# A fused two-branch attention kernel: where single maxima, the last output rows and their sums are placed

## The chip, the cores and the metric

The kernel runs on one core of one Trainium2 chip. The metric is the device time of one execution in microseconds (us); the median of several executions is given. A core has these engines, each with an instruction queue of its own, which they work through in order: TensorE (in the profile PE, with its weight loads as PEld), VectorE (DVE), ScalarE (ACT), GpSimd (POOL) and SyncE (SP, which here only issues transfers). They wait for each other through semaphores alone. Matmul results land in PSUM, eight banks of 128 partitions by 512 fp32 values; the other data lie in SBUF.

## The reference

The input x has 2048 tokens of 512 values. Two attention branches with 32 heads of 16 values work on the same x; a gate per token mixes them.

```python
# branch A: each query looks at 8 keys, at distances 0, 2, ... 14
qkv = (x @ wqkv).reshape(B, S, 3, H, Dh)
logits = einsum("bhsd,bhswd->bhsw", q, k[idx]) * scale      # masked where idx < 0
a = einsum("bhsw,bhswd->bhsd", softmax(logits), v[idx]).reshape(B, S, D) @ wo_a
# branch B: full attention, one key and value head shared by all 32 query heads
q = (x @ wq).reshape(B, S, H, Dh); k = x @ wk; v = x @ wv
p = softmax(einsum("bhqd,bkd->bhqk", q, k) * scale)
b = einsum("bhqk,bkd->bhqd", p, v).reshape(B, S, D) @ wo_b
g = sigmoid((x * gate_w).sum(-1))
out = g * a + (1 - g) * b
```

B_wq and B_wk are drawn eight times larger than the other weights. The scores of branch B are so large that the maximum of each row has to be taken off before the exponential.

## The kernel before

**The main loop.** Branch B is cut into 32 units: four blocks of 512 queries by eight groups of four heads. A unit has 16 steps, one for each 128 keys, so there are 512 steps s = 0 to 511 (`NS`), and one more that only finishes; `u, kt = divmod(s, 16)` gives unit and place in it. A step does `exp_pair(s, 0)` and `exp_pair(s, 1)`: two score products (L473) into one of the two double banks `pe` (`eb`), and one exponential of 128 x 1024 on ScalarE (L475). Then `weighted(s - 1)` (L483) multiplies the exponentials of the step before with the values into the bank `po`, which collects the sum of one unit. Score products use half of TensorE's rows each, so the two of a pair run side by side.

**The maxima.** Before a unit's exponentials start, the maxima of its score rows must be known, since they enter its queries as two further rows (L461, a transfer). They take 2048 half-array products in all, 64 a unit, with TensorE and VectorE working ahead of the exponentials. A *pair* (`fill_pair`, products at L324, reduction at L344) puts two products into the double bank `pm` (`m2`) and reduces 1024 values; a *single* (`fill_one`, reduction at L355) puts one product into the bank `ps` (`m1`). In the front part a third form is used, a *difference pair* (`fill_diff`, `fill_sum`): products of sums and differences of keys at L409, absolute values on ScalarE (L419), and one VectorE operation with a running maximum (L429); one pair of it does four products' worth of maxima for four half-array products. A unit's maxima are collected in a tile `mx`, first filled with the lowest number: in the front part by ScalarE (L318) when a unit is first touched, in the main loop by GpSimd (L315), there for the unit after it as well. Three such tiles rotate.

**The order.** All engines' instruction order is fixed when the program is built, by a planner with its own clocks (`clk`) and costs (`T_R` and the others). In a step the order is `(0, "m2", "m1", 1)`: first score products, a pair of maxima if `m2` is free by the planner's clock, a single if `m1` is free, second score products. Singles are used only while `singles(s)` holds, that is while more maxima are left than pairs alone would do by step 480, and not at a unit's first step (`kt` is 0): there `finish_a` also has VectorE transpose `po` (L497) and take reciprocals (L503) behind `weighted` of the unit that ended. If a unit's maxima are still missing shortly before it starts, `pause` runs what is left through the `pe` banks as well, without exponentials.

**The front.** Before the loop, `stream` runs the projections (`lumps`, products at L1057) on the banks `e0` and `e1` and fills maxima in between; the last lump uses `m2`. The set `ended` stops the filling of `m2` near the end of the lump before it.

**Output rows.** The last 512-wide products with wo_a and wo_b are made in four blocks of four row groups. Three blocks run as `out_phase` at a unit's second step, once branch A (GpSimd's work, `work`) is far enough, the block's units are shaped, and the maxima are less than `LEAD` = 3 units ahead. The last four row groups come in two parts: `spread` makes most of their products (L812, 21 slots of two for each row group, into `m2`) in the last steps of the loop, at most four slots a step (`spread_some`), after a preparation (`prepare` L637 and L639, transposes L783, splits L793 and L795). At the end of a row group ScalarE copies the second bank (L829) and VectorE adds the first (L831), which frees `m2`. The generator is made in the loop once unit 29 is shaped and no maxima are left. What needs the last unit's result comes after the loop in two halves x = 0, 1 (L1170 to L1188): transposes, normalisation, a split in two parts (L1177, L1178), six products, the sum with `parts[j]` (L1187), the store.

Of the kernel before, what the change touches and what calls it, by code (L numbers as in the profile page):

```python
# [6 lines left out]
F32 = mybir.dt.float32  # L7
# [11 lines left out]
NJ = S // P  # L19
C = D // P  # L20
# [28 lines left out]
def gated_mix_kernel(ctx, tc, xt, wa, wk, wq, wo_a, wo_b, out):  # L49
# [36 lines left out]
    def after(eng, ready, dur):  # L86
        clk[eng] = max(clk[eng], ready) + dur
        return clk[eng]
# [219 lines left out]
        return bool(half) or bool(slots) and slots[0][0] < len(stacked) and stacked[slots[0][0]] <= clk["pe"]  # L308

    def unit_tile(v):  # L310
        for x in (v, v + 1) if pe else (v,):
            if x < NU and x not in left:
                mx[x] = wp.tile([P, 2, 2, 4, 4], F32, name="mx", bufs=3)
                if pe:
                    nc.gpsimd.memset(mx[x], -FMAX)  # L315
                    charge(250)
                else:
                    nc.scalar.activation(mx[x].rearrange("p b i t k -> p (b i t k)"), ident[:, 0:64], AF.Identity, scale=0.0, bias=mk[:, 6:7])  # L318
                left[x] = NF // NU
        return mx[v]  # L320
# [455 lines left out]
    def spread(js, n):  # L776

        m = 3 * (C + n)

        def turn_all(j):  # L780
            bank = m1
            for c in range(C):
                nc.tensor.transpose(bank[:, c * P:(c + 1) * P], oa[c // 2][:, j, c % 2 * P:(c % 2 + 1) * P], ident)  # L783
            after("pe", 0, 0.7)
            own = p2[0].tile([P, C, P], F32, name="raw", bufs=1)
            nc.scalar.activation(own, bank.rearrange("p (c q) -> p c q", c=C), AF.Copy)
            after("act", clk["pe"] + T_LAT, 0.6)
            return own

        def parts_a(j, own):  # L790
            nonlocal pool
            hi, lo = turned[j, 0] = [pe[0].tile([P, C, P], F32R, name=f"turned{x}", bufs=1) for x in range(2)]
            nc.scalar.activation(hi, own, AF.Copy)  # L793
            at = after("act", clk["pe"], 0.6)
            nc.gpsimd.tensor_sub(lo, own, hi.bitcast(F32))  # L795
            pool = max(pool, 1e3 * at) + 1300

        prepare(js[0], n)
        yield 1.0
        parts_a(js[0], turn_all(js[0]))  # L800
        yield 3.0
        while slots or half:
            yield 1.0
        for j in js:
            nxt = j + 1 if j != js[-1] else None
            items = []
            for i in range(m):
                items = items or out_items(j, n)
                st, mv = items[i]
                for b in range(2):  # L810
                    h = slice(64 * b, 64 * b + 64)
                    nc.tensor.matmul(m2[:, b, :], st()[h], mv[h], start=(i == 0), stop=(i == m - 1))  # L812
                after("pe", 0, T_R)
                row_left[0] = m - 1 - i
                if i == 3 * n and nxt:
                    prepare(nxt, n)
                if i == m - 8 and nxt:
                    raw = turn_all(nxt)
                if i < m - 1:
                    yield 0.0  # L820
            del turned[j, 0], turned[j, 1]
            x = len(parts)
            if x < 2:
                spare.append(p2[0].tile([P, 512], F32, name="part", tag=("own", "tr8")[x], bufs=1))
            elif x == 2:
                two = p2[0].tile([P, 2, 512], F32, name="part", tag="pr", bufs=1)
                spare.extend([two[:, 0, :], two[:, 1, :]])
            parts[j] = spare[x]
            nc.scalar.activation(parts[j], m2[:, 1, :], AF.Copy)  # L829
            after("dve", after("act", clk["pe"] + T_LAT, 0.5), 0.7)  # L830
            nc.vector.tensor_add(parts[j], m2[:, 0, :], parts[j])  # L831
            if nxt:
                parts_a(nxt, raw)
            yield 1.5
        done.add("last")

    def spread_some(k):
# [222 lines left out]
    def done_mm(at):  # L1060
        nonlocal pool
        x, i = at
        lump = lumps[x]
        if i % 3 == 2:
            run_tasks()
            if p2:
                run_pool()
        if x == last - 1 and i == 3 * C - 2:
            ended.add(1)
        if x == last and i in (2, 7):  # L1070
            exp_pair(0, int(i == 2))
        if i < 3 * C - 1:
            return
        if lump[0] == "q":
            m = lump[1]
            queries_post(m, eb[x % 2])
            free[f"e{x % 2}"] = clk["act"]
            ahead_wa(0, m - 4)
        else:
            gg, j = lump[1:]  # L1080
            a_post(gg, j, 2 if x == last else x % 2)
            if gg + 1 < C:
                ahead_wa(gg + 1, j - 2)
# [22 lines left out]
    for s in range(NS + 1):  # L1106
# [16 lines left out]
        order = (0, "m2", "m1", 1) if s > 1 else (1, "m2", 0, "m1") if s else ()  # L1123
        k, n = outs // 4, C - (outs >= NJ - 4)
        if outs == NJ - 4:
            if NU - 3 in shaped and not half and not singles(s) and not later_rows and "last" not in done:
                later_rows.append(spread(list(range(outs, NJ)), n))
            if short > 0 and steps < 2:
                pause(short)
        elif due or outs < NJ and s and kt == 0 and outs // NH in done and NHG * (k + 1) - 1 in shaped and (lead < LEAD or s >= 16 * (NHG * (k + 2) + 1)):  # L1130
            if not due:
                prepare(outs, n)
                due.append(n)
            else:
                out_phase(list(range(outs, outs + 4)), due.pop(), kt == 1)
                outs += 4
                order = (0, "m1", 2)
        elif short > 0 and steps < 2:
            pause(short)

        for which in order:
            if which == "m2":
                fill_ready("m2", M2S)
            elif which == "m1":
                if not later_rows and (kt or not s) and singles(s):
                    fill_ready("m1", M1S)
            elif s < NS:
                exp_pair(s, which % 2 or which // 2, which == 2)
# [17 lines left out]
    for x in range(2):  # L1166
# [8 lines left out]
        nc.vector.transpose(own, obp["t"][:, 8 * x:8 * x + 8].rearrange("p b h d -> p (b h d)"))  # L1175
        tl = wp.tile([P, 2, 256], F32R, name=f"tl{x}", tag="aext", bufs=2)
        nc.scalar.activation(tl[:, 0], own, AF.Copy)  # L1177
        nc.gpsimd.tensor_sub(tl[:, 1], own, tl[:, 0].bitcast(F32))  # L1178
        tls.append(tl)
    for x in range(2):  # L1180
        for k, w in ((0, woh), (0, wol), (1, woh)):
            for t in range(2):
                nc.tensor.matmul(eb[x][:, t, :], tls[x][:, k, t * P:(t + 1) * P], w[1][:, C - 1, :], start=(w is woh and k == 0), stop=(k == 1))
        for t in range(2):
            j = NJ - 4 + 2 * x + t
            os = px.tile([P, D], F32, name="osl", tag="pexp", bufs=6)
            nc.vector.tensor_add(os, eb[x][:, t, :], parts[j])  # L1187
            (nc.sync, nc.scalar)[t].dma_start(out[0].rearrange("(p j) d -> p j d", j=NJ)[:, j, :], os)  # L1188
# [29 lines left out]
```

## Time and profile before

| | |
|---|---|
| median of three executions | 1504.08 us (1503.17 to 1506.13) |
| profiled execution | 1503.76 us, span 1502.0 us |
| mean granted TensorE clock | 0.997 |
| front part, up to the first product into po | 274.2 us |
| TensorE, share of the span | 98% |
| ScalarE | 86% |
| VectorE | 79% |
| GpSimd | 68% |

The span runs from the first to the last instruction; the profiled execution took 1.76 us more. A line of groups or of the timeline names the source line, the engine, the operation, the tile written and the tiles read, their shapes and the count; in brackets stands how long the engine was idle before it, and who released it. The busy time of matmuls is modelled at its ends, so that a busy TensorE is not at its peak rate; the distance from one start to the next tells more. The granted clock is the share of full speed that TensorE was given.

### The profile page before, as it was taken

The numbers are of one execution on the slowest core, as the hardware profiler recorded it, in microseconds if no ns is written. First come the engines' busy times: TensorE is split into PE (matmuls) and PEld (weight loads), VectorE is DVE, ScalarE is ACT, GpSimd is POOL, SyncE is SP. The second block draws the span as 40 slices with busy tenths as digits, with TensorE's granted clock in tenths as the row PEclk, the third lists the DMA queues.
The fourth block names the chain that finished last, engine by engine and source line by source line (L and its number), as shares of the span: only waits on it lengthen the run. The fifth ranks groups of instructions, "written<-read, shape, count | busy, mean of one in ns | idle before, by whom it ended". The sixth has DMA issues, their size and how long they took to land.

```text
span 1502.0 us, 29449 instructions
## 1 busy us (share of the span) xinstructions
PE 1479.2 (98%) x11020; PEld 710.5 (47%) x11020; DVE 1188.4 (79%) x1814; ACT 1285.7 (86%) x1672; POOL 1024.8 (68%) x1806
## 2 busy tenths in 40 slices
PE   9999999999999999999999999999999999999998
PEld 6899888433333333333733345333333463333343
DVE  6976666788888888888788888888888888888801
ACT  5568988899999999999899988999989889999785
POOL 7876988788888888988988799788897130111021
PEclk9999999999999999999999999999999999999999
DMA  6754223121120211211212112021120000000000
GB/s 219 212 147 143 76 87 117 33 83 46 60 84 12 73 58 41 70 41 41 69 41 70 41 41 87 12 70 41 41 76 16 12 30 12 2 1 2 1 2 28
DMA packets 44287, 87.75 MB, mean 58 GB/s; under 512 B 9520, under 2 KB 25952, under 8 KB 39920
## 3 DMA queue, kind: packets, MB, share of 16 engines
q1 hardware_dynamic: 37136, 46.89, 10.3%
q0 software_dynamic: 6432, 37.94, 7.5%
q8 instruction: 86, 1.41, 0.4%
q10 hardware_dynamic: 576, 1.05, 0.2%
q14 instruction: 57, 0.47, 0.1%
HBM read 59.02 MB, written 26.30 MB: 57 GB/s over the span
## 4 chain that ended last, share of the span: by engine, by line
PE 91%; ACT 5%; DVE 2%; issue 1%; DMA 0%; POOL 0%; SPq 0%; DVEq 0%; ACTq 0%; POOLq 0%
PE po L483 33%; PE pe L473 25%; PE pe L1057 8%; PE pm L324 8%; PE ps L324 5%; PE pe L740 4%; PE pm L409 2%; ACT dd L419 2%; ACT pexp L475 1%; PE ps L409 1%; PE pm L812 1%; PE po L409 1%; PE pe L183 1%; DMA xraw<-xt 0%; DVE mx L344 0%
## 5 line engine op out<-in xcount | busy, mean ns | idle before, releaser
L475 ACT ACTIVATE pexp<-pe 128x1024 f32<-128x1024 f32 x1021 | 987.3, 1023 | 106.0 <-PE pe L473 103.6
L344 DVE TENSOR_REDUCE mx<-pm 128x2 f32<-128x1024 f32 x508 | 620.0, 1221 | 147.4 <-PE pm L324 139.6
L483 PE MATMUL po<-pexp,vst 128*32 128x512 f32 x4096 | 546.6, 606 | 0.0
L473 PE MATMUL pe<-qst,kst 64*128 64x512 f32 x1914 | 520.4, 455 | 5.6 <-DVE mx L344 2.9
L473 PEld LDWEIGHTS pe<-qst,kst 64*128 64x128 f32 x1914 | 213.3, 184 | 424.6 <-ACT pexp L475 410.2
L355 DVE TENSOR_REDUCE mx<-ps 128x1 f32<-128x512 f32 x446 | 303.1, 680 | 2.1 <-PE ps L324 2.1
L324 PE MATMUL pm<-kst,qst 62*128 62x512 f32 x968 | 196.8, 398 | 2.9 <-DVE mx L344 2.1
L543 POOL TENSOR_TENSOR pr<-aext 128x256 f32<-128x256 f32 x256 | 182.6, 741 | 3.4 <-DMA aext<-ad 3.1
L324 PE MATMUL ps<-kst,qst 62*128 62x512 f32 x422 | 177.3, 420 | 0.5 <-DVE mx L355 0.3
L603 POOL TENSOR_TENSOR oa<-oa,av 128x256 f32<-128x256 f32 x224 | 164.5, 734 | 14.9
L483 PEld LDWEIGHTS po<-pexp,vst 128*32 128x32 f32 x4096 | 80.6, 108 | 174.5 <-issue 166.6
L600 POOL TENSOR_TENSOR av<-aext,lg 128x256 f32<-128x256 f32 x224 | 139.7, 623 | 12.5
L324 PEld LDWEIGHTS ps<-kst,qst 62*128 62x128 f32 x422 | 77.5, 184 | 68.3 <-DVE mx L355 64.9
L1057 PE MATMUL pe<-wah,xl 64*128 64x384 f32 (+1 forms) x504 | 108.9, 338 | 0.0
L419 ACT ACTIVATE dd<-pm 128x512 f32<-128x512 f32 x166 | 92.0, 608 | 19.6 <-PE pm L409 9.5
L1057 PE MATMUL pe<-wah,xh 64*128 64x384 f32 (+1 forms) x504 | 108.6, 337 | 0.0
L1057 PE MATMUL pe<-wal,xh 64*128 64x384 f32 (+1 forms) x504 | 108.3, 337 | 0.0
L429 DVE CUSTOM_DVE_ANT_0 dd<-ps,dd 128x512 f32<-128x512 f32 x83 | 57.4, 692 | 58.4 <-PE ps L409 25.4
L324 PEld LDWEIGHTS pm<-kst,qst 62*128 62x128 f32 x968 | 93.2, 187 | 8.0 <-DVE mx L344 3.4
L509 POOL TENSOR_TENSOR rl<-rl,gate_t 128x16 f32<-128x16 f32 x31 | 6.9, 222 | 118.2 <-DVE rl L503 118.1
L549 POOL TENSOR_TENSOR tr<-pr 128x512 f32<-128x512 f32 x64 | 81.7, 1277 | 4.1
L549 POOL TENSOR_TENSOR tr<-tr 128x256 f32<-128x256 f32 (+1 forms) x128 | 72.5, 567 | 9.0
(215 smaller groups left out, 1908.1 us busy)
## 6 DMA issues: line engine op xcount, KB each, us to landing
aext<-ad POOLq DMA_DIRECT2D x32, 1056.0 KB, 5.5
ad<-stage SPq DMA_DIRECT2D x32, 384.0 KB
qst<-qd SPq DMA_DIRECT2D x60, 128.0 KB
xraw<-xt SPq DMA_DIRECT2D x16, 256.0 KB
qd<-qhi SPq DMA_DIRECT2D x16, 256.0 KB
qd<-qlo SPq DMA_DIRECT2D x16, 256.0 KB
qst<-qd SPq DMA_DIRECT2D x60, 64.0 KB
qst<-ml SPq DMA_DIRECT2D x216, 2.0 KB
```

The lines of the kernel that those rows point to most:

```text
L324: nc.tensor.matmul(dst, qst[home(v)[0]][b:b + 62, pr, t * P:(t + 1) * P], kst[b:b + 62, kc * 512:(kc + 1) * 512], start=True, stop=True)
L344: nc.vector.tensor_reduce(m[:, :, pr, t, kc], dst, AX.X, ALU.max)
L355: nc.vector.tensor_reduce(m[:, odd, pr, t, kc:kc + 1], dst, AX.X, ALU.max)
L419: nc.scalar.activation(dd[0][:, odd], m2[:, odd, :], AF.Abs)
L473: nc.tensor.matmul(bank[:, odd, :], kst[b:b + 64, kt * P:(kt + 1) * P], qst[home(u)[0]][b:b + 64, pr, :], start=True, stop=True)
L475: nc.scalar.activation(e, bank, AF.Exp, scale=SCALE)
L483: nc.tensor.matmul(po[32 * i:32 * i + 32, :], vst[:, kt, :], pexp[s, i // 2][:, i % 2, :], start=(kt == 0), stop=(kt == NJ - 1))
L543: nc.gpsimd.tensor_mul(pr[:, k], q, e[:, o:o + NH, AC:2 * AC])
L549: nc.gpsimd.tensor_add(nx, cur[:, :, 0:n], cur[:, :, n:2 * n])
L600: nc.gpsimd.tensor_mul(av, e[:, o:o + NH, 2 * AC:].rearrange("p j (h d) -> p j h d", d=DH), lg[:, w].unsqueeze(3).to_broadcast([P, NH, AG, ...
L603: nc.gpsimd.tensor_add(ao, ao, av)
L1057: nc.tensor.matmul(front[2 if x == last else x % 2][0][:, b, :n], l[h], r[h], start=(i == 0), stop=(i == 3 * C - 1))
```

## The change

- A unit's first step may have a single of maxima too: `(kt or not s)` leaves the condition.
- The generator of the last rows is made once at most nine maxima products are left, not only when none is left. It prepares its first row group, and begins products when no maxima are left. Once it is made there are no singles.
- At the end of a row group VectorE copies the second bank and then adds the first; ScalarE does no copy. For the last row group ScalarE still copies, and VectorE's addition moves behind the loop, between the two halves of the tail.
- In the tail's second half VectorE does the subtraction of the split, not GpSimd.
- In the front part too, touching a unit fills the `mx` tile of the next one.
- In the last lump but one, the filling of `m2` stops at i = 6 and not at i = 10.

```diff
     def unit_tile(v):
-        for x in (v, v + 1) if pe else (v,):
+        for x in (v, v + 1):
             if x < NU and x not in left:
...
             parts[j] = spare[x]
-            nc.scalar.activation(parts[j], m2[:, 1, :], AF.Copy)
-            after("dve", after("act", clk["pe"] + T_LAT, 0.5), 0.7)
-            nc.vector.tensor_add(parts[j], m2[:, 0, :], parts[j])
             if nxt:
+                nc.vector.tensor_copy(parts[j], m2[:, 1, :])
+                nc.vector.tensor_add(parts[j], m2[:, 0, :], parts[j])
                 parts_a(nxt, raw)
-            yield 1.5
+                after("dve", clk["pe"] + T_LAT, 1.4)
+                yield 1.5
+            else:
+                nc.scalar.activation(parts[j], m2[:, 1, :], AF.Copy)
         done.add("last")
...
-        if x == last - 1 and i == 3 * C - 2:
+        if x == last - 1 and i == 3 * C - 6:
             ended.add(1)
...
-            if NU - 3 in shaped and not half and not singles(s) and not later_rows and "last" not in done:
+            if NU - 3 in shaped and to_go() <= 9 and not later_rows and "last" not in done:
                 later_rows.append(spread(list(range(outs, NJ)), n))
...
-                if not later_rows and (kt or not s) and singles(s):
+                if not later_rows and singles(s):
                     fill_ready("m1", M1S)
...
-        nc.gpsimd.tensor_sub(tl[:, 1], own, tl[:, 0].bitcast(F32))
+        (nc.vector if x else nc.gpsimd).tensor_sub(tl[:, 1], own, tl[:, 0].bitcast(F32))
         tls.append(tl)
+        if not x:
+            nc.vector.tensor_add(parts[NJ - 1], m2[:, 0, :], parts[NJ - 1])
```

## The prediction

> **What bounds the kernel now.** I read the page's totals and chain first, then busy time by stretches, then the timeline at the places that the change touches.
>
> ```profile
> PE 1479.2 (98%) x11020; PEld 710.5 (47%) x11020; DVE 1188.4 (79%) x1814; ACT 1285.7 (86%) x1672; POOL 1024.8 (68%) x1806
> PE 91%; ACT 5%; DVE 2%; issue 1%; DMA 0%; POOL 0%; SPq 0%; DVEq 0%; ACTq 0%; POOLq 0%
> ```
>
> TensorE is busy 98% of the 1502.0 us and carries 91% of the chain, so a matmul slot that is added costs time, and one that is filled sideways saves only idle time. The stretches (columns: time, then busy us and instructions of PE, PEld, DVE, ACT, POOL, then the granted clock, DMA) show where idle time is left:
>
> ```profile
> 274.00:1398.00 1124.00, 1120.03 (x7992) 439.49 (x7993) 961.09 (x1301) 1016.04 (x1155) 788.92 (x1468) 1.00 0.13 43
> 1417.50:1424.00 6.50, 3.29 (x20) 1.65 (x21) 5.09 (x6) 1.32 (x3) 0.00 (x0) 0.72 0.00 1
> ```
>
> In the main loop PE idles 4 us in 1124. One hole stands out: 1417.5 to 1424, where the unfinished maxima of the last unit are forced and PE is busy 3.29 of 6.50. What surrounds it, PE's timeline:
>
> ```profile
> 1398.61 0.50 PE L473 MATMUL pe<-qst,kst 64*128 64x512 f32 x2
> 1400.50 0.50 PE L473 MATMUL pe<-qst,kst 64*128 64x512 f32 x2
> 1402.65 0.50 PE L473 MATMUL pe<-qst,kst 64*128 64x512 f32 x2
> 1404.54 0.50 PE L473 MATMUL pe<-qst,kst 64*128 64x512 f32 x2
> 1417.45 0.50 PE L324 MATMUL pe<-kst,qst 62*128 62x512 f32 x1
> 1422.13 0.80 PE L473 MATMUL pe<-qst,kst 64*128 64x512 f32 x2 [2.90 <-DVE mx L344]
> ```
>
> The L473 rows open steps 480, 481, 482 and 483. Steps 480 (a unit's first) and 482 have a pair of maxima and no single: 1.89 us each. The six steps 483 to 488 have pair and single: (1417.45 - 1404.54) / 6 = 2.15. A single so costs 0.26 us, as much PE time as a pair, which does two maxima. At 1417.45 the forced maxima start; PE resumes 4.68 us later, after 2.90 idle. The idle has a second price, in the one-microsecond stretches (PE busy, then the clock):
>
> ```profile
> 1426.00:1427.00 1.00, 1.00 (x8) 0.50 0.00 0
> 1427.00:1428.00 1.00, 1.00 (x10) 0.89 0.00 0
> ...
> 1432.00:1433.00 1.00, 0.43 (x6) 1.00 0.00 0
> ```
>
> The clock is at half until 1427, so the restart is slow too; at 1432 PE is busy 0.43 of a microsecond and keeps the full clock. How many maxima are left comes from L324 and L409 alone (first three rows L324, the last L409; the first bracket is PE's count):
>
> ```profile
> 0.00:714.00 714.00, 160.53 (x691) 85.69 (x691) 1.00 0.28 86
> 1398.00:1417.40 19.40, 5.36 (x25) 2.97 (x25) 1.00 0.01 2
> 1417.40:1424.00 6.60, 2.10 (x9) 1.00 (x9) 0.73 0.00 1
> 0.00:714.00 714.00, 98.10 (x332) 47.05 (x332) 1.00 0.28 86
> ```
>
> So 34 of 2048 are left at step 480, and 9 when they are forced.
>
> **Part 1: singles at first steps.** Steps 16, 32, ... 464 are 29 steps that had a pair alone. The rule for singles asks that more maxima are left than pairs can do by step 480; with 34 left there it held throughout, and with some 29 fewer it still holds nearly to the end. 29 x 0.26 = **+7.5 us**. Whether VectorE can carry it is read at a unit's end (PE, then DVE):
>
> ```profile
> 1364.85 0.50 PE L473 MATMUL pe<-qst,kst 64*128 64x512 f32 x2
> 1366.76 0.50 PE L473 MATMUL pe<-qst,kst 64*128 64x512 f32 x2
> 1369.24 0.40 PE L324 MATMUL pm<-kst,qst 62*128 62x512 f32 x2
> 1365.64 1.23 DVE L344 TENSOR_REDUCE mx<-pm 128x2 f32<-128x1024 f32 x1 [0.31 <-PE pm L324]
> 1366.89 0.72 DVE L497 STREAM_TRANSPOSE tt<-po 128x512 f32<-128x512 f32 x1
> 1367.65 0.26 DVE L503 RECIPROCAL rl<-tt 128x16 f32<-128x16 f32 x1
> 1367.82 1.17 DVE L344 TENSOR_REDUCE mx<-pm 128x2 f32<-128x1024 f32 x1
> 1368.89 0.68 DVE L355 TENSOR_REDUCE mx<-ps 128x1 f32<-128x512 f32 x1
> 1371.59 1.23 DVE L344 TENSOR_REDUCE mx<-pm 128x2 f32<-128x1024 f32 x1 [0.68 <-PE pm L324]
> ```
>
> The added reduction (0.68, some 0.60 behind starts that overlap) stands ahead of the transpose of po. Behind it wait the transpose (po's next product), the reciprocal, and the next pair, whose reduction ends at 1368.99 and frees pm. With it that is 1369.59, while PE, itself 0.26 later, wants pm at 1369.50. The transpose would end near 1368.1; po's next product is due 2.15 less po's own 1.07 (a row below) behind that step's start at 1366.76 + 0.26, so at 1368.1 as well. The stall is so some 0.05 to 0.1 a unit; I take 0.05, **+1.5 us** in all. Bounds: nothing, if the overlap is as large as in the best pair of rows, and 0.27 a unit (+8), if it were 0.68 with a reduction of branch A (0.2 more) always in between. By step 18 the planner leaves a single out already (VectorE is behind in its own costs too), and the wait of 0.68 ahead of step 19's pair shows that the backlog ends there. So each unit gains one single net.
>
> The planner's lead at step 208 is (691 + 332) / 64 - 13 = 2.98 units, just under the 3.0 that lets the first block of output rows start. Twelve more maxima (+0.19) put it over: the first two blocks should start a unit later, same work, 0 us.
>
> **Part 2: the last front lump.** Filling stops at i = 6 of the lump before it, not 10, which drops one difference pair (ACT, PE):
>
> ```profile
> 268.94 1.08 ACT L419 ACTIVATE dd<-pm 128x512 f32<-128x512 f32 x2 [0.60 <-PE pm L409]
> 270.08 0.45 PE L1057 MATMUL pm<-wah,xh 64*128 64x384 f32 x2 [0.83 <-ACT dd L419]
> ```
>
> The last lump takes the bank that this pair held, and waits 0.83 for ScalarE's 1.08 of absolute values. Without it that wait, two slots on PE and the 1.08 ahead of the first exponentials go: between 0.8 and 1.5, and since ScalarE paces the first steps I take **-1.1 us**. The four maxima of the pair move to the main loop: 34 - 29 + 4 = 9 are left at step 480.
>
> **Part 3: first values a unit ahead.** In the front the first touch of a unit now fills two tiles with -FMAX, so unit 1's are there early (ACT, DVE, PE):
>
> ```profile
> 41.19 0.33 ACT L318 ACTIVATE mx<-ident,mk 128x64 f32<-128x64 f32 x1
> 41.55 1.23 DVE L344 TENSOR_REDUCE mx<-pm 128x2 f32<-128x1024 f32 x1 [2.88 <-ACT mx L318]
> 42.84 0.50 PE L324 MATMUL pm<-kst,qst 62*128 62x512 f32 x2 [1.85 <-DVE mx L344]
> ```
>
> ScalarE reached this fill late; VectorE waited 2.88 for it and PE 1.85 for VectorE. The earlier fill puts 0.33 more into ScalarE's queue before the first pair. PE's wait goes: **-1.85 us**. It is nothing, or +0.3, if the queue around it (GpSimd's splits of the queries) holds PE at the same point; late next would be ScalarE's copy of the bank, so the full amount is nearer to the row.
>
> **Part 4: the end.** The rows that bear on it (ACT, PE):
>
> ```profile
> 1431.70 3.75 ACT L475 ACTIVATE pexp<-pe 128x1024 f32<-128x1024 f32 x4
> 1447.03 0.60 ACT L829 ACTIVATE part<-pm 128x512 f32<-128x512 f32 x1
> 1425.57 1.22 PE L473 MATMUL pe<-qst,kst 64*128 64x512 f32 x4
> 1432.76 0.49 PE L473 MATMUL pe<-qst,kst 64*128 64x512 f32 x2 [0.57 <-ACT pexp L475]
> 1448.41 0.97 PE L812 MATMUL pm<-woh,own 64*128 64x512 f32 x6 [0.25 <-DVE part L831]
> 1487.32 0.50 PE L812 MATMUL pm<-wol,turned 64*128 64x512 f32 x2
> 1488.68 1.07 PE L483 MATMUL po<-pexp,vst 128*32 128x512 f32 x8
> ```
>
> Before, step 480 to the end of the last po is 1489.75 - 1398.61 = 91.1. After, 9 maxima at step 480 are gone in three steps (2.15 + 2.15 + 1.89 = 6.2). Unit 29 has its shape when step 482 ends, so the rows' generator starts at 483 instead of 490, and nothing has to be forced. Its preparation takes three steps, as from 1425.57 to 1432.76: 7.2. The rows' first 19 steps took 1487.32 - 1432.76 = 54.6; the twentieth now has exponentials too, 1.63 of PE (1.89 less a slot) plus five slots of 0.26, 2.9. At three row borders VectorE copies and adds (some 0.65 + 0.69) without waiting for ScalarE's queue; the 0.25 that PE waits each time goes: 54.6 + 2.9 - 0.75 = 56.8. Then six steps have nothing beside the exponentials. ScalarE sets them: 3.75 for four, some 0.915 apart, so 12 x 0.915 = 11.0, with 0.8 of lead-in and 1.07 of po: 12.9. ScalarE's copy of the last row fits its idle time. Sum 83.1, that is **-8.0 us**. Bounds: -5, if preparation beside maxima and ScalarE's queue cost a step more, and -10, if the bare steps overlap better.
>
> The last rows' final sum moves between the two halves of the tail: it leaves the way of the first, delays the second by its 0.69, and the subtraction that goes from GpSimd to VectorE saves about as much: 0 us, from -0.4 to +0.5. Two rows bear on that (DVE, POOL):
>
> ```profile
> 1492.39 0.68 DVE L1173 TENSOR_TENSOR rll<-rll,gate_t 128x8 f32<-128x8 f32 x1
> 1492.32 0.73 POOL L1178 TENSOR_TENSOR tl<-ttl,tl 128x256 fp32r<-128x256 f32 x1 [13.73 <-ACT tl L1177]
> ```
>
> The multiplication of eight columns lasts 0.68 and ends with GpSimd's subtraction beside it. The Trainium skill (SBUF — State Buffer, "Who interferes with whom") says that a VectorE operation with two SBUF inputs and a GpSimd operation lock each other out for a whole instruction; the trace agrees. By that rule the second subtraction, now VectorE's own, can't lock it out, and the tail gains up to 0.5; if the first still meets the multiplication, it gains nothing.
>
> **The sum.** 7.5 + 1.5 - 1.1 - 1.85 - 8.0 + 0 = -1.95. The profiled execution took 1503.76 (1.76 around the span), so 1501.8; the median shown is 0.3 above it: 1502.1. 0.2% is 3.0 us, about what a measurement of this kernel can tell from no change.
>
> **Rivals.** (a) Slower: VectorE's order decides. If reduction and transpose at a unit's end delay PE by 0.3 instead of 0.05, 29 units give 8.7 instead of 1.5, and the time is 1509. It decides from 0.05 + 5.0 / 29 = 0.22 a unit (1502.1 to 1507.1). For it: 0.68 more ahead of a transpose that po waits for. Against: VectorE is clear again by step 19.
> (b) The gains come in full: no stall (-1.5), the tail gains 0.5, the bare steps hide (-1): 1499. For it: the 4 us of idle time in the whole loop, little of which is at unit ends.
> (c) The change doesn't do what it says: the planner, with VectorE busier in its costs, leaves out another single in each unit. Then the 7.5 + 1.5 fall away, the forced maxima and their idle time stay (-8.0 shrinks to the borders' -0.75), and 1.1 + 1.85 + 0.75 are gained: 1500.3. Against: one left-out step a unit covers the backlog.
> (d) The six bare steps lose the clock: PE's 1.63 a step becomes 3.3 against ScalarE's 1.83, some +9, 1511. Against: full clock at 1432 with PE busy 0.43; the gaps in bare steps are 0.2. The Trainium skill (TensorE: Matmul & The Clock Gate, Part 1) asks for an idle window of about 3.4 us before the clock halves; the half clock here began in the 2.9 us hole, and by that rule gaps of 0.2 leave it full.
>
> **Chances.** Forecast as summed, within 0.2%: 0.43. (b) 0.27 and (c) 0.10: faster, 0.37. (a) 0.16 and (d) 0.04: slower, 0.20. The forecast's own range, with the terms' bounds, is 1499 to 1505; the range for 8 in 10 reaches to most of (b) and toward (a): 1497.5 to 1507.5.
>
> **What would show it.** Twenty-nine more single maxima between 274 and 1398 and a pair with a single in each unit's first step at 2.15; pm at the unit's third step waiting for VectorE by under 0.1; no half clock before the end; no wait for L318 near 41 and none for dd in the last front lump; the rows' products beginning seven steps earlier than now, and six steps of 1.83 behind them. The prediction is wrong if unit ends stall by more than 0.2, if the forced maxima remain, or if the bare steps last over 2.

## The result and the profile after

The changed kernel takes 1510.97 us (median), beside 1504.91 for the kernel before: the ratio is 1.0042, with a 95% interval of 1.0028 to 1.0056. It is slower by about 6 us, where 1502.1 was forecast. The profiled execution took 1510.97 as well, 1509.2 of it span: 7.2 more than before's 1502.0.

The totals and the shares of the chain, of after:

```profile
PE 1484.5 (98%) x11020; PEld 710.6 (47%) x11020; DVE 1193.7 (79%) x1822; ACT 1280.1 (85%) x1660; POOL 1021.5 (68%) x1804
PE 88%; ACT 5%; POOL 2%; DVE 2%; issue 2%; DMA 1%; SPq 0%; DVEq 0%; ACTq 0%; POOLq 0%
```

TensorE is as full as it was, but only 88% of the chain is its own (91% before): GpSimd and a transfer now have a share of 2% and 1%. Four stretches show where the 7.2 us lie: the front up to the loop's first score product (L473), the loop from there to step 480, the end from step 480 to the last product into po, and the tail. The columns are those of the prediction's stretches. Before:

```profile
0.00:270.94 270.94, 264.16 (x2370) 229.15 (x2372) 192.79 (x463) 196.17 (x432) 217.62 (x315) 1.00 0.47 142
270.94:1398.61 1127.67, 1123.52 (x8024) 441.77 (x8022) 962.96 (x1306) 1019.19 (x1158) 791.90 (x1471) 1.00 0.13 43
1398.61:1489.75 91.14, 86.17 (x615) 36.17 (x611) 26.28 (x33) 69.51 (x81) 13.81 (x19) 0.96 0.01 1
1489.75:1502.00 12.25, 5.39 (x20) 3.45 (x20) 6.36 (x15) 0.83 (x2) 1.47 (x2) 0.87 0.23 86
```

After:

```profile
0.00:269.98 269.98, 262.42 (x2367) 231.93 (x2368) 192.74 (x461) 192.56 (x430) 216.62 (x314) 1.00 0.46 141
269.98:1415.05 1145.07, 1134.78 (x8039) 440.81 (x8037) 974.16 (x1320) 1018.56 (x1152) 790.27 (x1471) 1.00 0.13 42
1415.05:1498.60 83.55, 81.92 (x602) 34.41 (x598) 20.31 (x27) 68.17 (x78) 13.85 (x19) 1.00 0.01 1
1498.60:1509.20 10.60, 5.34 (x21) 3.45 (x20) 6.51 (x16) 0.83 (x2) 0.74 (x1) 0.95 0.27 99
```

Where step 480 begins is found by counting the products into po, eight a step; VectorE's transpose of the finished unit in the same step fits it (DVE, after):

```profile
1417.57 0.70 DVE L497 STREAM_TRANSPOSE tt<-po 128x512 f32<-128x512 f32 x1
```

| stretch | predicted | measured |
|---|---|---|
| front | -2.95 | -0.96 |
| loop | +9.0 | +17.4 |
| end | -8.0 | -7.6 |
| tail | 0 | -1.65 |
| sum | -1.95 | +7.2 |

In the loop TensorE's busy time grew by 11.3 (some of it at half clock) and its idle time from 4.15 to 10.29. Most of the idle time is one hole. ScalarE, then TensorE, of after:

```profile
446.14 0.63 ACT L81 ACTIVATE woh<-os 128x512 fp32r<-128x512 f32 x1 [4.38 <-DMA os<-wo_b]
447.74 0.79 PE L473 MATMUL pe<-qst,kst 64*128 64x512 f32 x2 [4.31 <-ACT pexp L475]
```

The stretch behind it, in the columns of the stretches (the clock is the third number from the end):

```profile
446.70:453.40 6.70, 5.67 (x22) 2.61 (x22) 3.33 (x5) 4.84 (x6) 5.80 (x8) 0.50 0.03 7
```

ScalarE splits a piece of wo ahead of step 79's exponentials and waits 4.38 us for its load. TensorE waits 4.31 for those exponentials, and then runs at half clock for nearly 7 us. Who issued what, in order of time, in before and then in after (SP's queue carries the eight shift transfers and the loads of wo, GpSimd the 1 MB load of branch A):

```profile
432.75 5.30 SPq L461 DMA_DIRECT2D qst<-ml  x8
438.15 2.74 SPq L625 DMA_DIRECT2D os<-wo_b  x2
438.60 0.59 POOL L532 DMA_DIRECT2D aext<-ad  x1
440.78 0.63 ACT L81 ACTIVATE woh<-os 128x512 fp32r<-128x512 f32 x1
```

```profile
434.05 5.29 SPq L461 DMA_DIRECT2D qst<-ml  x8
439.18 0.59 POOL L532 DMA_DIRECT2D aext<-ad  x1
439.45 2.23 SPq L625 DMA_DIRECT2D os<-wo_b  x2
```

Before, the load of wo (256 KB) went out 0.45 ahead of the large one, and the split began 2.63 behind it without a wait. After, it goes out 0.27 behind the large one, and lands 6.7 later (439.45 to 446.14).

The front: the wait for L318 near 41 is gone, and so is the 0.83 in the last lump, but two new ones have come. TensorE of after:

```profile
196.23 0.51 PE L409 MATMUL pm<-kcd,qst 62*128 62x512 f32 x2 [1.61 <-ACT dd L419]
229.28 0.51 PE L409 MATMUL pm<-kcd,qst 62*128 62x512 f32 x2 [1.93 <-ACT dd L419]
```

What holds the absolute values (L419) is the copy ahead of them in ScalarE's queue. ScalarE, SP and GpSimd of after, then the same of before:

```profile
227.37 0.49 ACT L249 ACTIVATE stage<-pe 128x384 f32<-128x384 f32 x1 [2.36 <-PE po L409]
221.39 0.38 SPq L266 DMA_DIRECT2D ad<-stage  x1
221.35 0.57 POOL L532 DMA_DIRECT2D aext<-ad  x1
```

```profile
226.07 0.49 ACT L249 ACTIVATE stage<-pe 128x384 f32<-128x384 f32 x1 [0.18 <-POOL stage L259]
222.14 0.38 SPq L266 DMA_DIRECT2D ad<-stage  x1
222.19 0.58 POOL L532 DMA_DIRECT2D aext<-ad  x1
```

The copy writes one of two buffers, which is free when its store (SP, L266) is out. Before, the store went out 0.05 ahead of a 1 MB load, after 0.04 behind it. That order does not decide it: two of the kernels below, b_only_singles and b_only_end, have the front of the kernel before as it was, their stores go out 0.06 and 0.08 ahead of the load, and ScalarE waits 2.53 and 2.47 there. What makes the store late in one execution and not in another stays open, and the profile of before is of an execution without such a wait. The profile names a product of TensorE as the releaser; the runs below show that it was the store.

The end has no forced maxima, no pause and no half clock, but it starts with 21 maxima left, not 9, and the products of the rows begin at 1434.07, in step 488: five steps earlier than before (step 493) and not seven. How many maxima were done in the loop (L324, then L409) in before and in after, and what was left in after:

```profile
270.94:1398.61 1127.67, 299.20 (x1358) 164.96 (x1358) 1.00 0.13 43
270.94:1398.61 1127.67, 63.77 (x220) 30.89 (x220) 1.00 0.13 43
```

```profile
269.98:1415.05 1145.07, 312.30 (x1391) 171.43 (x1391) 1.00 0.13 42
269.98:1415.05 1145.07, 58.40 (x204) 28.44 (x204) 1.00 0.13 42
1415.05:1434.00 18.95, 4.72 (x21) 2.42 (x21) 1.00 0.00 1
```

Singles brought 30 and pairs 3, and the filling beside the output rows, which uses the difference form L409, lost 16; with the four moved from the front, 34 + 4 - 33 + 16 = 21. Four bare steps (508 to 511) remain instead of the six forecast, at 1.95 us from start to start; the first product of the rows, then the exponentials of the bare steps and the waits for them (PE, ACT, PE), of after:

```profile
1434.07 0.96 PE L812 MATMUL pm<-woh,own 64*128 64x512 f32 x6
...
1489.69 3.77 ACT L475 ACTIVATE pexp<-pe 128x1024 f32<-128x1024 f32 x4
1491.68 0.50 PE L473 MATMUL pe<-qst,kst 64*128 64x512 f32 x2 [0.41 <-ACT pexp L475]
1495.69 0.49 PE L473 MATMUL pe<-qst,kst 64*128 64x512 f32 x2 [0.25 <-ACT pexp L475]
1497.54 1.06 PE L483 MATMUL po<-pexp,vst 128*32 128x512 f32 x8 [0.35 <-ACT pexp L475]
```

### The profile page after: what moved, and what is told of

It is laid out like the page before. It is cut to its first block, busy times and chain, and to the rows that moved or that the text cites. A ratio compares the mean times of both kernels' runs of the same rounds, so it can differ in the third digit from the quotient of the medians.

```text
span 1509.2 us, 29437 instructions
## 1 busy us (share of the span) xinstructions
PE 1484.5 (98%) x11020; PEld 710.6 (47%) x11020; DVE 1193.7 (79%) x1822; ACT 1280.1 (85%) x1660; POOL 1021.5 (68%) x1804
## 4 chain that ended last, share of the span: by engine, by line
PE 88%; ACT 5%; POOL 2%; DVE 2%; issue 2%; DMA 1%; SPq 0%; DVEq 0%; ACTq 0%; POOLq 0%
PE po L483 32%; PE pe L473 25%; PE pm L324 8%; PE pe L1059 6%; PE ps L324 4%; PE pe L740 4%; PE pm L409 2%; ACT pexp L475 2%; ACT dd L419 2%; PE pm L812 1%; PE ps L409 1%; PE po L409 1%; POOL qlo L220 1%; POOL qraw L213 1%; PE pe L183 1%
## 5 line engine op out<-in xcount | busy, mean ns | idle before, releaser
L473 PE MATMUL pe<-qst,kst 64*128 64x512 f32 x1914 | 532.9, 455 | 7.4 <-ACT pexp L475 7.2
L473 PEld LDWEIGHTS pe<-qst,kst 64*128 64x128 f32 x1914 | 219.8, 185 | 414.4 <-ACT pexp L475 404.8
L355 DVE TENSOR_REDUCE mx<-ps 128x1 f32<-128x512 f32 x473 | 321.4, 680 | 4.1 <-PE ps L324 4.1
L324 PE MATMUL pm<-kst,qst 62*128 62x512 f32 x964 | 199.9, 404 | 1.4 <-ACT pexp L475 0.8
L324 PE MATMUL ps<-kst,qst 62*128 62x512 f32 x447 | 189.2, 423 | 0.5 <-DVE mx L355 0.3
L324 PEld LDWEIGHTS ps<-kst,qst 62*128 62x128 f32 x447 | 82.4, 184 | 77.0 <-DVE mx L355 74.2
L419 ACT ACTIVATE dd<-pm 128x512 f32<-128x512 f32 x164 | 90.8, 610 | 17.8 <-PE pm L409 10.8
L324 PEld LDWEIGHTS pm<-kst,qst 62*128 62x128 f32 x964 | 94.7, 188 | 9.5 <-DVE mx L344 4.3
```

What stands on the lines that cost most here:

```text
L324: nc.tensor.matmul(dst, qst[home(v)[0]][b:b + 62, pr, t * P:(t + 1) * P], kst[b:b + 62, kc * 512:(kc + 1) * 512], start=True, stop=True)
L355: nc.vector.tensor_reduce(m[:, odd, pr, t, kc:kc + 1], dst, AX.X, ALU.max)
L419: nc.scalar.activation(dd[0][:, odd], m2[:, odd, :], AF.Abs)
L473: nc.tensor.matmul(bank[:, odd, :], kst[b:b + 64, kt * P:(kt + 1) * P], qst[home(u)[0]][b:b + 64, pr, :], start=True, stop=True)
```

## The experiments

Theory at the start: the singles cost the loop some 10 us and give the end less; the wait for wo and the waits for the stores are accidents of timing that the singles or the front's edits bring about. Rivals: that the hole near 443 has another cause than a late load, or that the loss is in the new end. The table gives the same four stretches for every kernel, read from the rows that bound them, and the times; the interval is that of the ratio to the kernel before, run beside it. The kernels ran in groups, with medians of the kernel before of 1505.1 (a_no_singles, b_only_singles, a_early_wo, b_only_end), 1506.6 (b_only_front, c_best, c_best_stage, d_end_stage) and 1506.1 (the others); where two kernels of different groups are compared by their times, a microsecond is not to be relied on. The expectations take step 480 one step early in the kernels whose load is late, so that their 1142.9, 6.35 and 1133.5 for the loop are some 2.1 too low, and what they call steps 80 to 88 is step 79 by the count of products into po.

| kernel | front | loop | end | tail | median | ratio (95%) |
|---|---|---|---|---|---|---|
| before | 270.9 | 1127.7 | 91.1 | 12.2 | 1504.9 | |
| after | 270.0 | 1145.1 | 83.6 | 10.6 | 1511.0 | 1.0028 to 1.0056 |
| b_only_singles | 277.5 | 1138.1 | 84.4 | 12.0 | 1511.2 | 1.0022 to 1.0046 |
| a_no_singles | 271.6 | 1136.1 | 88.6 | 10.8 | 1510.0 | 1.0019 to 1.0037 |
| a_early_wo | 269.9 | 1137.9 | 83.8 | 10.6 | 1505.9 | 0.9992 to 1.0011 |
| b_only_end | 275.9 | 1127.5 | 88.6 | 10.6 | 1503.4 | 0.9969 to 0.9990 |
| b_only_front | 272.9 | 1135.7 | 90.8 | 12.6 | 1513.5 | 1.0025 to 1.0054 |
| b_only_mx | 274.8 | 1128.3 | 91.0 | 12.3 | 1508.0 | 0.9996 to 1.0019 |
| b_only_lump | 271.4 | 1135.7 | 90.8 | 12.6 | 1513.0 | 1.0033 to 1.0061 |
| a_swap | 271.8 | 1141.1 | 83.6 | 10.6 | 1510.1 | 1.0014 to 1.0047 |
| c_best | 271.6 | 1129.0 | 87.9 | 10.8 | 1504.6 | 0.9962 to 0.9993 |
| c_best_stage | 265.8 | 1129.0 | 89.1 | 10.8 | 1496.6 | 0.9913 to 0.9953 |
| d_end_stage | 270.6 | 1125.5 | 94.0 | 10.6 | 1503.1 | 0.9966 to 0.9991 |
| a_mended | 265.9 | 1137.8 | 83.8 | 10.6 | 1500.0 | 0.9933 to 0.9971 |
| b_mended | 272.0 | 1125.5 | 94.0 | 14.6 | 1506.9 | 0.9992 to 1.0016 |
| c_no_lump | 267.5 | 1125.7 | 94.0 | 10.6 | 1499.8 | 0.9932 to 0.9970 |
| c_late_singles | 269.6 | 1133.7 | 83.7 | 10.8 | 1495.9 | 0.9908 to 0.9949 |

**a_no_singles**, the change without Part 1:

```diff
-                if not later_rows and singles(s):
+                if not later_rows and (kt or not s) and singles(s):
```

> The changed kernel with the old rule for singles (none at a unit's first step); the other three parts stay. Theory: the 27 added singles cost 27 x 0.26 = 7.0 us plus some 3 us of stalls on TensorE, and they move the load of wo behind a large load, which costs 4.4 us at steps 80 to 88. Without them the main loop from step 0 to 480 is back at about 1127.7 to 1128 us (1142.9 with them), more than 30 maxima are left at step 480, the pause for them comes back, and the end keeps only what the borders (-0.75) and the tail (-1.65) save; the front keeps its -0.96: 1510.97 - 1504.91 = +6.1 becomes about -2 to -3, that is 1502 to 1503. Rival A: the wait at steps 80 to 88 has another cause than the singles and stays: some 1506.5. Rival B: the loss lies in the front or the end: the time stays at 1510.

Measured 1509.95: the time is that of rival B, but the loss is in the loop, which is 1136.1, 8.5 above before, and the hole is there (5.61 us of waiting for wo). So rival A had the cause right: the singles didn't bring the late load. Taking them out makes the loop 9.0 shorter and the end 5.1 longer, and gains only 1 us in time.

**b_only_singles**, Part 1 alone on the kernel before, by the reverse of that edit:

> The kernel before with the singles at the units' first steps alone. Theory: the main loop grows by 29 x 0.26 = 7.5 us and some 3 us of stalls, the end gives back what the pause costs (half clock and idle, some 4 us) where fewer maxima are left. Without a late load of wo that is +5 to +8 over the kernel before, 1510 to 1513; with the load late again, 4.4 more, up to 1517. Rival: the stalls and the late load come from the front's new timing, then only 7.5 - 4 = +3.5, some 1508.5.

Measured 1511.21. The loop grows by 10.5 and the end shrinks by 6.7; 33 more singles (447 against 414) cost 10.5 / 33 = 0.32 each. No wait for wo. Its front is 6.5 longer than in the profile of before, though the program there is the same: two waits for stores (2.38 and 2.53) and two stretches of half clock. The rest, 10.5 - 6.7, is what Part 1 costs net.

**a_early_wo**, the change with each split of wo one item later in the list of pieces (the loads stay in their items):

```diff
-    for i in range(2 * C + 1):
-        wos.append([(wo_load, kcs[i])] if i < 2 * C else [])
-        wos[-1] += [(wo_split, kcs[i - 1])] if i else []
+    for i in range(2 * C + 2):
+        wos.append([(wo_split, kcs[i - 2])] if i > 1 else [])
+        wos[-1] += [(wo_load, kcs[i])] if i < 2 * C else []
```

> The changed kernel with each split of wo put one item of the list later, so that its load has an item's time more to land. Nothing is left out. Theory: the wait of 4.4 us at step 86 and the half clock behind it are a late load alone; they go, and the time is 1510.97 - 4.4 = 1506.6 (between 1506 and 1507.5). Rival: TensorE runs into the next stall at the same place (VectorE's backlog), and the gain is under 1 us: 1510.

Measured 1505.88, a little under the span expected and 5.1 less than the changed kernel. The wait and the half clock behind it are gone, the loop is 7.2 shorter, and 16 maxima are left at step 480 instead of 21. The products of the rows begin in step 486, seven steps earlier than before, and six bare steps follow. The theory holds: a late load is what made the hole.

**b_only_end**, Part 4 alone (the singles' rule, the first values and the last lump as before):

> The changed kernel with the singles' rule, the front's first values and the last front lump all as before: the end's part alone (rows begun at 9 maxima left or fewer, VectorE alone for the sums, the new tail). Theory: main loop as before (1127.7), 34 maxima left at step 480, so the pause for the maxima stays; the rows can begin one or two steps earlier beside the last maxima, the borders save 0.75 and the tail 1.65: 1504.91 - 2.4 = 1502.5, 1501.5 at best. Rival: the changed sums on VectorE delay the maxima or the exponentials and give that back: 1505.

Measured 1503.40, as the theory had it: loop as before, end -2.5, tail -1.65. The new end isn't where the loss is.

**b_only_front**, Parts 2 and 3 alone on the kernel before:

```diff
-        for x in (v, v + 1) if pe else (v,):
+        for x in (v, v + 1):
...
-        if x == last - 1 and i == 3 * C - 2:
+        if x == last - 1 and i == 3 * C - 6:
```

> The kernel before with the front's two edits alone (first values a unit ahead, the last front lump's fill stopped earlier). Theory, after the run without the singles: these two edits, and not the singles, move the 1 MB load of branch A ahead of the load of wo at step 85. The front is about 1 us shorter at most (the 2.95 predicted are given back where ScalarE waits for a store near 194 and 227), the main loop is 4 to 6.5 us longer, the end as before: 1505.1 + 3 to 5.5, that is 1508 to 1510.5. Rival: the order of the two loads comes from the end's edit or from the two together; then the loop is as before (1127.7) and the time is 1502 to 1504.

Measured 1513.47. The loop is 1135.7, so the front's edits do turn the two loads round; the loss is larger than expected, since the front waits for stores as well (2.16 and 3.13 us) and is 2 us longer than before's, not shorter.

**b_only_mx** and **b_only_lump**, each of the two lines alone:

> The kernel before with the first values a unit ahead alone. The loads keep their order if the last lump's edit turned it round: the loop is 1127.7 then, the front 1 to 3 us shorter (the rest given back at the stores), and the time 1502 to 1504. If this edit turned it round, the loop is 1133.5 and the time 1509 to 1511.

> The kernel before with the last front lump's edit alone. If this edit turns the order of the two loads round, the loop is 1133.5 and the time 1509 to 1511, as with both edits; if not, the front is 1.7 us shorter, the loop as before, and the time 1503 to 1505.

The lump's edit is the one: 1512.98 and a loop of 1135.7, against 1508.02 and 1128.3. SP, GpSimd and ScalarE of b_only_lump:

```profile
439.37 0.59 POOL L532 DMA_DIRECT2D aext<-ad  x1
441.15 0.84 SPq L625 DMA_DIRECT2D os<-wo_b  x2
446.00 0.63 ACT L81 ACTIVATE woh<-os 128x512 fp32r<-128x512 f32 x1 [5.81 <-DMA os<-wo_b]
```

A difference pair dropped at 268 us so costs some 7 us at 441: the order of the loads that GpSimd and SP issue there is another one. How the planner comes to that order was not followed. b_only_mx missed its 1502 to 1504 for another reason, three waits for stores in the front (1.89, 1.64 and 1.90), which eat all that the first values gain.

**a_swap**, the change with the 1 MB load issued behind the pieces of wo:

```diff
-            yield from load(i + 3)
             for _ in range(2):
                 if p2b and extra:
                     for f, a in extra.pop(0):
                         f(*a)
                     yield 1300
+            yield from load(i + 3)
```

> The changed kernel with GpSimd's loads for branch A issued behind the pieces of wo instead of ahead of them; the splits of wo stay where they were. Theory: the load of wo is late because the 1 MB load goes out 0.27 us ahead of it and shares its DMA engines; with that load behind it, the split waits for nothing, and the time is as with the later split, 1506 (1505 to 1507.5). Rival: 256 KB need more than the 2.6 us between load and split whatever is beside them; then the wait stays, and the time is 1510 or more.

The wait is halved, which neither theory nor rival had. SP, GpSimd and ScalarE of a_swap:

```profile
440.92 2.21 SPq L625 DMA_DIRECT2D os<-wo_b  x2
445.44 0.59 POOL L532 DMA_DIRECT2D aext<-ad  x1
443.52 0.63 ACT L81 ACTIVATE woh<-os 128x512 fp32r<-128x512 f32 x1 [2.14 <-DMA os<-wo_b]
```

With no large load ahead of it the load takes 2.6 us (440.92 to 443.52), with one ahead 4.85 (b_only_lump) to 6.7 (after). What is left, 2.14, is that ScalarE reaches the split 0.46 behind the issue of its load (440.92, behind the eight shift transfers in SP's queue): the split before it, at 440.76, stands right ahead of it there, where before and after have two exponentials in between. So two things make the load late for its split: the large load that goes out ahead of it, and the place of load and split in their queues. The Trainium skill (DMA: Bandwidth & Descriptors, "Issuing engines are not separate DMA queues") says that transfers from different engines end up on the same 16 DMA engines and interleave; the three durations agree. The loop is 3.9 shorter than after's, but the front is 1.85 longer with one more wait for a store (2.08 at 140.6), and the median, 1510.07, hides the gain.

**c_best**, the change without the singles and with the splits one item later:

> The changed kernel without the singles at first steps, and with each split of wo one item of the list later. Theory: nothing waits for wo, the loop is as before (1127.5), the front at -1 to +0.6, the end at -0.4 to -2.5 and the tail at -1.65: a_no_singles less its 6.35 us in the loop, 1503.6, between 1501.5 and 1504. Rival: splits that come later push GpSimd's branch A, and the loop stays 2 us or more above before: 1506.

Measured 1504.63, a little above the expected span of values; the loop is 1129.0, near the 1127.5 expected. The executions range from 1499.9 to 1507.7.

**c_best_stage**: the same with a third buffer for the stores of the front, in a part of oa that is written only later:

```diff
-            stage["t"] = p1.tile([P, GC, 2, AN], F32, name="stage", bufs=2)
+            stage["t"] = oa[0][:, 12:15, :].rearrange("p a n -> p (a n)").rearrange("p (g x n) -> p g x n", g=GC, x=2) if (gg * NJ + j) // 2 % 3 == 2 else p1.tile([P, GC, 2, AN], F32, name="stage", bufs=2)
```

> As the run before it (no singles at first steps, splits of wo later), with a third buffer for the stores of the front (in a part of oa that is not yet in use). Theory: ScalarE's waits for a store at 194 and 227, 1.6 and 1.9 us on TensorE, and the half clock that sometimes follows them, go; the front is 268 us or shorter up to the first exponentials (270 to 271.6 with the waits) and the time falls by 3 to 4.5: about 1500. Rival: another wait takes their place (the absolute differences on ScalarE, GpSimd's adds), and the gain is under 1 us.

Measured 1496.60, 8.0 below c_best where 3 to 4.5 were expected, and five of six executions lie within 0.3 us. What L249 waited for (us, times) in c_best:

```profile
  PE pe L1059: 8.5, 10
  DMA ad<-stage: 5.2, 3
```

In c_best_stage the row of the stores is not there any more, and the front's row changes as follows (c_best, then c_best_stage):

```profile
0.00:271.57 271.57, 263.66 (x2366) 232.21 (x2368) 192.87 (x461) 192.57 (x430) 216.50 (x314) 0.99 0.46 140
```

```profile
0.00:265.79 265.79, 260.77 (x2367) 230.94 (x2369) 192.70 (x461) 192.59 (x430) 216.50 (x314) 1.00 0.47 143
```

So the stores are what ScalarE waited for, and they make most of the scatter between executions. This kernel is 0.67% faster than the one before.

**d_end_stage** (the same with the front's edits taken back) and **c_no_lump** (only the lump's edit taken back) price Parts 2 and 3 where no store is waited for:

> As the run before it (third store buffer, splits of wo later, the new end, no singles at first steps), but with the front's two edits taken back. It prices the two edits where no store is waited for. By the prediction's terms (1.85 + 1.1) the front to the first exponentials is 2.95 us longer than in the run before it, and the time too: 1503 against 1500. Rival: the queue around the first pair holds TensorE anyhow, and the difference is 1.1 or less.

> c_best_stage with the last front lump's fill as before, so of the front's two edits only the first values a unit ahead. It splits the 4.83 us that the two were worth together. Theory from the offsets of equal products: 3.0 for the first values, 1.8 for the lump, so the front ends at 267.6 and the time is 1498.4. Rival, by the prediction's terms: the lump 1.1, so 1497.7.

Fronts of 270.62, 267.48 and 265.79: the first values are worth 3.1, the lump 1.7, more than either theory or rival of d_end_stage gave (2.95 or less for both; 4.8 measured). In time the first values are worth 1503.12 - 1499.75 = 3.4 and the lump 1499.75 - 1496.60 = 3.15; the latter's second half isn't in the front: without the edit the loop is 3.3 shorter, and the end 4.9 longer, with fewer maxima filled beside the output rows (208 products of the difference form in the loop, and 216 with it). The times, 1503.12 and 1499.75, are near the expected 1503 and above the 1498.4.

**a_mended**, the whole change with both mends (splits later, third buffer):

> The whole change, singles at first steps too, with the two waits mended that it ran into: each split of wo one item of the list later, and a third buffer for the front's stores. Theory: it is c_best_stage and the singles, which cost some 9 us in the loop (1138 instead of 1129) and give back 5.3 at the end (83.8 instead of 89.1): 1496.6 + 3.7 = 1500.3. The terms of the prediction, whose sum had no such waits, gave 1502.1. Rival: the singles' cost in the loop was part of the waits, and the time is that of c_best_stage, 1496.6, or below.

Measured 1500.02. Against c_best_stage the singles cost 8.8 in the loop and give back 5.3 at the end, 3.4 net. Loop and end of a_mended:

```profile
265.85:1403.62 1137.77, 1133.46 (x8045) 440.48 (x8043) 973.85 (x1331) 1021.58 (x1158) 792.21 (x1471) 1.00 0.13 43
1403.62:1487.42 83.80, 81.38 (x597) 33.71 (x593) 17.20 (x23) 68.07 (x78) 13.88 (x19) 1.00 0.01 1
```

**b_mended**, both mends on the kernel before:

> The kernel before with the same two mends and nothing of the change. Theory: in its profile ScalarE hardly waited for a store and not for wo, so its time moves little, but the executions no longer scatter over 1503 to 1512: 1503 to 1504.5 in nearly all. Rival: the scatter has another source and stays.

Measured 1506.88 where 1503 to 1504.5 was expected. The executions do lie closer (1506.3 to 1508.1, those of before beside them 1503.6 to 1512.2), but the end is 2.9 longer (43 maxima left, not 34), and the profiled tail 2.4 longer. So the mends alone are worth nothing; they pay with Parts 2 to 4.

**c_late_singles**, c_best_stage with singles at the first steps of the last 14 units alone:

```diff
-                if not later_rows and (kt or not s) and singles(s):
+                if not later_rows and (kt or not s or s > 240) and singles(s):
```

> c_best_stage with singles at the first steps of the last 14 units alone (steps 256 to 464). Theory: 14 x 0.33 = 4.6 us in the loop; some 23 maxima are left at step 480 instead of 37, so nothing is forced, and the pause with its half clock (2.9 idle and up to 3.4 of lost clock) goes: the end is 84.5 instead of 89.1. No gain and no loss: 1496.6, from 1495.5 to 1498. Rival: the pause stays, and the time is 1500.

Measured 1495.93, the fastest of all, 0.71% below the kernel before. 15 more singles than in c_best_stage cost 4.7 in the loop and take 5.3 off the end: the pause is gone for half the price. The stretches are those of its slowest execution (1499.57), whose front has a wait of 3.38 near 35 us that the other profiles don't have. Its lead of 0.7 on c_best_stage was not measured side by side, and is small.

## Why the prediction was wrong

**Part 1** (+9.0 in the loop) was sized about right: 8.8 (a_mended against c_best_stage) to 10.5. Singles rose by 30 (414 to 444). In a_mended a unit's first step takes 2.16 where it took 1.90, and its third 2.00 where it took 1.90 (medians over the units); so VectorE's order costs 0.10 a unit and not 0.05, and stays under the 0.22 from which rival (a) would have decided. That the two first output blocks start a unit later came true. "Same work, 0 us" holds nearly in a_early_wo, where the blocks start at the same steps: the filling beside them shrank by 4 products. In the changed kernel it shrank by 16; why the late load's kernel fills fewer is not shown.

**Part 2** (-1.1) is the step that failed most. In the front the edit is worth 1.7. The step priced it there alone, and did not follow the dropped pair into the order of the work afterwards: it turns the loads at 439 us round, and costs the loop some 7 us (7.2 between after and a_early_wo, 7.1 between a_no_singles and c_best). The margin could have been read beforehand: the split began 2.63 behind the issue of its load and without idle time, and the 1 MB load went out only 0.45 behind that of wo.

**Part 3** (-1.85) was right about the mechanism; where nothing takes it back it is worth 3.1. The sentence that failed is "late next would be ScalarE's copy of the bank": the copy that was late next is L249, through its buffer's store, and in the changed kernel it returns some 4.1 (269.98 against 265.85 in a_mended). That the kernel before shows no such wait in its profile was luck: the same front waits in b_only_singles and b_only_end, where it lasts 277.5 and 275.9.

**Part 4** (-8.0) was sized right: -7.6, and -7.3 in a_early_wo and a_mended, where the load is in time. There 16 maxima are left at step 480, not 9, but the rows' products do begin seven steps earlier, and six bare steps of 1.97 (1.83 forecast) stand behind them in a_early_wo. In the changed kernel itself, with 21 maxima left and four bare steps, that the number fits is luck.

**The tail** (0, from -0.4) was mis-sized: -1.65, and between 10.6 and 10.8 in every kernel that has it. The step looked at VectorE's sums alone. The second multiplication by the gates does take less (DVE, then POOL, after):

```profile
1501.64 0.17 DVE L1175 TENSOR_TENSOR rll<-rll,gate_t 128x8 f32<-128x8 f32 x1
1500.96 0.74 POOL L1180 TENSOR_TENSOR tl<-ttl,tl 128x256 fp32r<-128x256 f32 x1 [23.52 <-ACT tl L1179]
```

It took 0.68 beside GpSimd's subtraction before. That subtraction is still there, but the moved sum puts the multiplication behind it. By the rule of the Trainium skill that the prediction quoted (SBUF — State Buffer, "Who interferes with whom") there is no lock without the neighbour; the rows agree. But the moved sum takes 0.65, and the last sum ends 7.63 behind the last product into po before and 7.50 after, so all this gains 0.13. The rest is in a closing instruction of GpSimd's queue, the longest of its three called DRAIN (shortest, median and longest in ns, then first and last start; before, then after):

```profile
L1215 POOLq DRAIN  x3: 46/102/6833, 1494.4 to 1501.7; - x3
L1219 POOLq DRAIN  x3: 46/102/6828, 1500.9 to 1508.9; - x3
```

It lasts 6.83 (6.8 to 7.2 in the other kernels) and starts as GpSimd comes to its last subtraction: 4.62 behind the last product into po before, 2.33 after, since VectorE has the second subtraction. Before, the span ends 0.78 behind it, and so do, within 0.01, the spans of all six kernels with the old tail (b_mended too, where it starts at 6.98 and the tail is 14.6). With the new tail the span ends 1.35 to 1.46 behind it, so that something else is last there; SP, which waits for the stores at the end, is the likely one.

Rivals (c) and (d) did not happen: the pause went, and the clock stayed full in the bare steps. The sum of the prediction's own terms describes the kernel without the two waits to 2 us: 1500.0 measured for a_mended, 1502.1 forecast; there the front and the tail gain 2.1 and 1.65 more than forecast, the loop and the end lose 1.1 and 0.7. What it lacked is two waits of ScalarE for transfers, 7.2 in the loop and 4.1 in the front: 11.3, and the spans of after and a_mended differ by 11.2.

## What to carry to other kernels

When an edit drops or moves work on engines that are planned in one go, look for the places later in the program where a transfer lands just in time, and ask what happens if it goes out half a microsecond later, behind a larger one. A gain in a stretch is real only when the next thing in that queue isn't a buffer that waits for its store; two small mends turned a change of +6 us into one of -6. And fill idle slots only as far as the pause they prevent: half of the singles bought all of the gain at the end. At the end of a kernel, look which engine's queue closes last: taking the last subtraction from GpSimd gained some 1.5 us that no sum of busy times had shown.

## What was not expected of the hardware

A hole of the same length halves TensorE's clock in one execution and not in another. The same wait for L318 near 41, 1.85 in before and 1.84 in b_mended; the stretch of the hole and the one behind it, the clock being the third number from the end, before and then b_mended:

```profile
40.90:42.70 1.80, 0.09 (x2) 0.00 (x0) 1.15 (x2) 0.62 (x2) 1.72 (x2) 1.00 0.55 141
43.10:46.40 3.30, 3.30 (x30) 2.47 (x30) 3.30 (x6) 1.66 (x2) 3.03 (x3) 1.00 0.77 216
```

```profile
40.90:42.70 1.80, 0.00 (x0) 0.00 (x0) 1.28 (x2) 0.49 (x2) 1.72 (x2) 1.00 0.56 146
43.10:46.40 3.30, 3.30 (x18) 2.60 (x16) 3.06 (x5) 1.52 (x2) 2.71 (x3) 0.50 0.77 219
```

18 matmuls run there instead of 30. The Trainium skill (TensorE: Matmul & The Clock Gate, Part 1) asks for an idle window of about 3.4 us; here a hole of 1.84 was enough in two of the six kernels whose profiles have it (b_mended and b_only_end), so gaps well below that are not safe. Such a hole can cost about twice its length, and whether it does differs from execution to execution.
